# One attention and gated-MLP kernel on one core: the planner that writes out its order gets a model of the DMA link

## The chip, the cores and the metric

The kernel runs on one core of one Trainium2 chip. The metric is the device time of one execution in microseconds (us). Its engines are TensorE (PE, with its weight loads as PEld), VectorE (DVE), ScalarE (ACT), GpSimd (POOL) and SyncE (SP). Each runs its own instructions in the order in which they stand. SP and POOL also issue the transfers (DMA), so a transfer's place in the order of its queue decides when it can start.

## The reference, cut to what matters

```python
# q, k, v: (8, 8, 576, 64); s: (8, 8, 576)
scores = scale * np.matmul(q, k.transpose(0, 1, 3, 2))
cum = np.cumsum(np.maximum(s, 0.0), axis=-1)
bias = -(cum[:, :, :, None] - cum[:, :, None, :])
scores = np.where(causal, -1e9, scores + np.minimum(bias, 0.0))
attn = softmax(scores)                       # with 1e-9 added to the sum
x = heads joined of np.matmul(attn, v)       # (8, 576, 512)
h = np.maximum(x @ w_in, 0.0)                # (8, 576, 1024)
u, v = h[..., :512], h[..., 512:]
v_n = (v - mean(v)) / np.sqrt(var(v) + 1e-6)
v_s = np.einsum('ts,bsd->btd', w_spatial, v_n) + b_spatial
out = (u * v_s) @ w_out
```

## The kernel before, in words

Every matrix product is made of float16 products: an operand is split into a high and a low half, and three products (high-high, high-low, low-high) are added in PSUM. The 64 heads are worked as 32 pairs, four pairs to a batch entry. For each pair `s_pass` makes the scores in seven or eight groups of matmuls, masks them and finds the smallest negated score on VectorE, takes exponentials on ScalarE, and splits the weights into `pb` (two heads of 4 blocks of rows each) and `pbt` (the last 64 rows of both heads). A DMA transpose on SP's queue turns each into `pT` (2 buffers' worth per pair, 4 buffers) and `pTt`. `av_pass` multiplies them with V: 30 + 30 matmuls into the one bank `psV`, 30 into `psT`. The four pairs of a batch entry fill `xt`, on which `mlp` does four stages: `xt` by the second half of `win` with a layer norm over features, the first half of `win`, the spatial product (`vn` by `ws`) and the output product (`g` by `wo`).

Pairs 0 to 2 take q and k as float32 ("native", in the tiles `g` and `xt`). For pairs 3 to 31 `load_raw` fetches `raw` on POOL's queue (576 KB), and `split_raw` makes the halves: ScalarE writes `KA`, GpSimd writes `QB` by subtraction, and SP's queue does five copies. In the order of the program they are `QA <- KA`, `KB <- KA`, `KB <- QB`, `QB <- KA`, and last the prefix sums `KA <- dr_cc`. `QB <- KA` overwrites the half of `QB` that `KB <- QB` reads, and `KA <- dr_cc` overwrites three rows of `KA` that `QB <- KA` reads, so each stands on SP's queue until the one before it has landed, and what is behind it stands too. The weights come in through POOL's queue too (`fetch_win`, 512 KB each) into buffers that later hold other things (`vn`, `g`, `u`, `wst`), and are taken apart on VectorE.

No instruction's place is written by hand. `Recorder.add` records each operation with a cost from `Recorder.cost` (time on its engine, `occ`, and time until its result is there, `lat`) and its predecessors from `Recorder.touch`. `Recorder.schedule` is a list scheduler: it walks a modelled clock, takes on each engine the ready operation of the lowest `prio` (a position that the plan at the end of `attn_gated_mlp` gives: scores of pair p at 2p, its `av_pass` at 2p + 3.7, the MLP of batch b from 8b + 10.3), and the order in which it took them is the order of each engine's instructions. The modelled clock is used for nothing else: on the chip only the order and the semaphores count. Since all instructions are issued by the wrapper, they carry one line number (L247).

Of the kernel before, what the change touches and what calls it, by code (L numbers as in the profile page):

```python
# [24 lines left out]
BYTES = {F32: 4, U32: 4, F16: 2, BF16: 2}  # L25
# [4 lines left out]


class Op:
    __slots__ = ("eng", "calls", "occ", "lat", "port", "preds", "succs", "prio", "n")


class Recorder:
    WAKE = {"vector": 30, "scalar": 30, "tensor": 50, "gpsimd": 85, "sync": 60}

    def __init__(self):
# [38 lines left out]
    def add(self, eng, method, args, kw):  # L78
        merge = isinstance(self.open, Op)
        if merge:  # L80
            op = self.open
            assert op.eng == eng
        else:
            op = Op()
            op.eng, op.calls, op.occ, op.lat, op.port = eng, [], 0.0, 0.0, False
            op.preds, op.succs, op.n = {}, [], len(self.ops)
            op.prio = self.prio
            self.ops.append(op)
            if self.open == "new":
                self.open = op  # L90
        op.calls.append((method, args, kw))
        is_ap = lambda x: hasattr(x, "ap") and hasattr(x, "tensor")
        writes = [x for k, x in kw.items() if k in ("out", "accum_out") and is_ap(x)]
        reads = [x for k, x in kw.items() if k not in ("out", "accum_out") and is_ap(x)]
        if args:
            rest = [x for x in args if is_ap(x)]
            if "out" in kw:
                reads += rest
            else:
                writes.append(rest[0])  # L100
                reads += rest[1:]
        occ, lat, port = self.cost(eng, method, writes, reads, kw, op)
        op.lat = max(op.lat, op.occ + lat)
        op.occ += occ
        op.port = op.port or port
        for w, aps in ((False, reads), (True, writes)):
            for ap in aps:
                r = self.region(ap)
                if r is not None:
                    self.touch(op, r, w)  # L110

    def touch(self, op, r, w):
        name, p0, p1, f0, f1 = r
        log = self.access.setdefault(name, [])
        kept = []
        for e in log:
            q0, q1, g0, g1, other, ow = e
            hit = q0 < p1 and p0 < q1 and g0 < f1 and f0 < g1
            if hit and (w or ow) and other is not op:
                data = ow and not w  # L120
                op.preds[other] = op.preds.get(other, False) or data or other.eng != op.eng
            if w and p0 <= q0 and q1 <= p1 and f0 <= g0 and g1 <= f1 and other is not op:
                continue
            if not w and not ow and other is op and e[:4] == (p0, p1, f0, f1):
                continue
            kept.append(e)
        kept.append((p0, p1, f0, f1, op, w))
        self.access[name] = kept

    def cost(self, eng, method, writes, reads, kw, op):  # L130
        size = lambda ap: ap.size() // ap.shape[0]
        n = max([size(a) for a in writes + reads] or [1])
        ps = any(a.tensor.name in self.psum for a in reads)
        point = any(size(a) == 1 for a in reads) and n > 1
        if method == "dma_start_transpose":
            return 1.26 * n + 60, 1.26 * n + 60 + 2500, False
        if method == "dma_start":
            b = max(a.size() * BYTES[a.dtype] for a in writes)
            o = 600
            return o, o + (2300 if eng == "sync" else 2800) + b / 180.0, False  # L140
        if eng == "tensor":
            n = size(writes[0])
            f32 = reads[0].dtype == F32
            t = n * (4 if f32 else 1) / 2.4 + 2.5
            t = max(t, 27.0)
            w = writes[0]
            key = (size(w), self.region(w)[1], w.shape[0])
            last = getattr(op, "calls")[-2:-1]
            if last and w.shape[0] == 64 and key[1] == 64:
                lw = last[0][1][0]  # L150
                if size(lw) == n and lw.shape[0] == 64 and self.region(lw)[1] == 0:
                    t = 3.0
            return t, t + 180, False
        if eng == "vector":
            if method == "tensor_tensor_reduce":
                return n / .96 + 76, n / .96 + 200, False
            if method == "reciprocal":
                return 85, 172, False
            if method == "bn_aggr":
                return 98, 180, False  # L160
            if method == "bn_stats":
                return n / .96 + 72, n / .96 + 152, False
            if n <= 16:
                return 75, 155, False
            big = [a for a in reads if size(a) > 16]
            if method == "memset":
                return n / .96 + 10, n / .96 + 80, False
            if method in ("tensor_copy", "tensor_scalar") and not ps:
                o = n / 1.92 + (195 if point else 75)
                return o, o + 80, True  # L170
            o = n / .96 + (130 if point and not ps else 72)
            return o, o + 80, len(big) > 1 and not ps
        if eng == "scalar":
            o = n / 1.2 + (50 if ps else 98) + (90 if point else 0)
            if len(writes) > 1:
                return o + 93, o + 200, False
            return o, o + 95, False
        if eng == "gpsimd":
            if method == "tensor_tensor":
                o = 560 if n < 16 else n * 1.9 + 150  # L180
            elif method == "memset":
                o = n * .86 + 80
            else:
                o = 260 if n < 16 else n * .9 + 150
            return o, o + 90, True
        raise ValueError((eng, method))

    def schedule(self):


        left = {}
        for op in self.ops:
            left[op] = len(op.preds)
            for p in op.preds:
                p.succs.append(op)
        free = dict.fromkeys(self.WAKE, 0.0)
        soon = {e: [] for e in free}
        ready = {e: [] for e in free}
        start = {}
        at = dict.fromkeys(self.ops, 0.0)  # L200
        port = 0.0
        for op in self.ops:
            if not left[op]:
                heapq.heappush(soon[op.eng], (0.0, op.n, op))
        order = []
        while len(order) < len(self.ops):
            best = None
            for e in free:
                t = free[e]
                while soon[e] and soon[e][0][0] <= t:  # L210
                    _, _, op = heapq.heappop(soon[e])
                    heapq.heappush(ready[e], (op.prio, op.n, op))
                if not ready[e]:
                    if not soon[e]:
                        continue
                    t = soon[e][0][0]
                    if best is not None and t >= best[0]:
                        continue
                if best is None or t < best[0]:
                    best = (t, e)  # L220
            t, e = best
            while soon[e] and soon[e][0][0] <= t:
                _, _, op = heapq.heappop(soon[e])
                heapq.heappush(ready[e], (op.prio, op.n, op))
            _, _, op = heapq.heappop(ready[e])
            s = t
            if op.port:
                s = max(s, port)
                port = s + op.occ
            start[op] = s  # L230
            free[e] = s + op.occ
            order.append(op)
            for o in op.succs:
                data = o.preds[op]
                when = s + op.lat + self.WAKE[o.eng] if data else s + 1
                at[o] = max(at[o], when)
                left[o] -= 1
                if not left[o]:
                    heapq.heappush(soon[o.eng], (at[o], o.n, o))
        self.start = start  # L240
        return order
# [612 lines left out]
```

## Time and profile before

| | |
|---|---|
| median of 3 runs | 744.07 us (741.94 to 750.85) |
| the profiled execution: time, span | 744.18 us, 742.5 us |
| granted TensorE clock, mean | 0.915 |
| PE busy | 619.3 us (83%) |
| DVE busy | 555.7 us (75%) |
| ACT busy | 516.0 us (69%) |
| POOL busy | 189.6 us (26%) |
| DMA moved | 119.30 MB, mean 161 GB/s |
| SP's queue, share of 16 DMA engines | 58.6% |
| POOL's queue, share of 16 DMA engines | 17.2% |

A busy share is an average over a start of about 240 us, in which weights and the first pairs come in, and a long middle in which TensorE is nearly full. So the table is read by stretches. "Issue to landing" of a transfer runs from its issue on the queue to the semaphore that says it is there.

### The profile page before, as it was taken

How to read it: one execution, taken by the hardware profiler on the slowest of the kernel's cores; microseconds unless marked ns; L12 is line 12 of the kernel's file. 1: busy time of each engine (PE TensorE's matmuls, PEld its weight loads, DVE VectorE, ACT ScalarE, POOL GpSimd, SP SyncE). 2: the span in 40 equal slices, each digit the busy share in tenths (PEclk: the TensorE clock that was granted, in tenths of full speed). 3: DMA queues.
4: the chain of work that ended last, by engine and by line, in shares of the span. 5: the costliest groups of instructions: out<-in, count | busy, mean ns of one | idle time of the engine just before them, and what ended most of it. 6: DMA issues, size and time to landing. Idle time of an engine off the chain costs nothing.

```text
span 742.5 us, 15798 instructions
## 1 busy us (share of the span) xinstructions
PE 619.3 (83%) x5696; PEld 427.1 (58%) x5696; DVE 555.7 (75%) x1602; ACT 516.0 (69%) x1328; POOL 189.6 (26%) x303
## 2 busy tenths in 40 slices
PE   4605445898559898998997999989999989999997
PEld 2202223466336476756775667657765777677676
DVE  7818697868966697978994988788877988984331
ACT  4626667566868496977895888778886978783322
POOL 7404223311422321233121331232233212100100
PEclk9857555989759999999998999999999999999999
DMA  8897677738679898898889687968897779564101
GB/s 227 244 164 172 145 154 163 174 63 180 174 142 213 185 163 183 173 226 159 193 171 190 137 197 160 255 141 184 153 241 170 180 144 196 100 115 87 43 2 64
DMA packets 237413, 119.30 MB, mean 161 GB/s; under 512 B 213864, under 2 KB 217110, under 8 KB 237335
## 3 DMA queue, kind: packets, MB, share of 16 engines
q1 hardware_dynamic: 228039, 83.23, 58.6%
q0 software_dynamic: 9296, 35.07, 17.2%
q8 instruction: 44, 0.72, 0.4%
q14 instruction: 34, 0.28, 0.1%
HBM read 37.48 MB, written 9.66 MB: 63 GB/s over the span
## 4 chain that ended last, share of the span: by engine, by line
PE 46%; DMA 16%; DVE 12%; ACT 8%; issue 2%; SPq 0%; POOL 0%; ACTq 0%; DVEq 0%; POOLq 0%
PE psM L247 33%; DMA pT<-pb 11%; PE psV L247 6%; PE psS L247 5%; DMA pTt<-pbt 3%; DVE psS L247 3%; ACT pb L247 2%; DVE pb L247 2%; PE psT L247 2%; DVE g L247 2%; ACT p L247 2%; DMA st<-st 1%; DVE pbt L247 1%; ACT q L247 1%; DVE st L247 1%
## 5 line engine op out<-in xcount | busy, mean ns | idle before, releaser
L247 DVE SCALAR_TENSOR_TENSOR pb<-p,sm,pb 128x384 f16<-128x384 f32 (+3 forms) x256 | 139.6, 582 | 36.5 <-ACT pb L247 35.9
L247 DVE CUSTOM_DVE_ANT_0 psS<-psS,mb 128x128 f32<-128x128 f32 (+2 forms) x295 | 142.6, 495 | 17.8 <-PE psS L247 14.0
L247 ACT ACTIVATE pb<-p,sm 128x384 f16<-128x384 f32 (+3 forms) x256 | 127.3, 553 | 30.5 <-DMA pT<-pb 17.8
L247 POOL TENSOR_TENSOR QB<-raw,KA 128x288 f16<-128x288 f32 x116 | 90.6, 807 | 207.5 <-ACT KA L247 207.2
L247 ACT ACTIVATE p<-psS,mx 128x128 f32<-128x128 f32 (+1 forms) x236 | 123.0, 527 | 29.4 <-DVE sm L247 17.6
L247 PEld LDWEIGHTS <-V 128*64 128x64 f16 x1920 | 82.6, 123 | 83.5 <-issue 73.8
L247 PE MATMUL psV<-pT,V 128*64 128x128 f16 (+2 forms) x960 | 78.7, 313 | 52.5 <-DMA pT<-pb 52.5
L247 PE MATMUL psM<-ws,vn 128*128 128x288 f16 x768 | 107.0, 287 | 0.0
L247 PE MATMUL psS<-KA,QA 128*128 128x512 f16 (+1 forms) x336 | 80.1, 315 | 29.4 <-ACT q L247 14.9
L247 PE MATMUL psM<-xt,win 128*128 128x288 f16 x768 | 101.1, 288 | 3.9 <-ACT u L247 3.6
L247 PE MATMUL psM<-g,wo 128*128 128x288 f16 x768 | 103.0, 288 | 1.6 <-DVE g L247 1.6
L247 PE MATMUL psM<-win,xt 128*128 128x512 f16 (+1 forms) x576 | 102.4, 354 | 0.8 <-ACT hv L247 0.5
L247 PEld LDWEIGHTS <-win 128*128 128x128 f16 x768 | 74.6, 98 | 27.0 <-issue 5.6
L247 PEld LDWEIGHTS <-wo 128*128 128x128 f16 x768 | 74.8, 98 | 25.1 <-issue 2.4
L247 PEld LDWEIGHTS <-vn 128*128 128x128 f16 x768 | 74.0, 98 | 24.3 <-issue 2.1
L247 PE MATMUL psS<-KB,QB 128*128 128x512 f16 (+1 forms) x336 | 87.1, 312 | 0.0
L247 PEld LDWEIGHTS <-xt 128*128 128x128 f16 (+1 forms) x576 | 48.0, 105 | 48.3 <-issue 6.5
L247 ACT ACTIVATE xt<-psV 128x512 f16<-128x512 f32 x32 | 19.1, 596 | 54.2 <-PE psV L247 54.2
L247 POOL TENSOR_SCALAR rs<-mv 128x1 f32<-128x1 f32 x40 | 8.8, 221 | 182.4 <-DVE mv L247 118.4
L247 PEld LDWEIGHTS <-QB 128*128 128x128 f16 x348 | 30.1, 105 | 41.1 <-issue 30.7
L247 DVE SCALAR_TENSOR_TENSOR xt<-psV,xt 128x512 f16<-128x512 f32 x32 | 21.9, 685 | 39.9 <-ACT xt L247 39.7
L247 ACT ACTIVATION_READ_ACCUMULATOR p<-psS,mx 128x1 f32 x236 | 47.8, 203 | 0.0
(112 smaller groups left out, 894.6 us busy)
## 6 DMA issues: line engine op xcount, KB each, us to landing
raw<-in_qkT_dram POOLq DMA_DIRECT2D x29, 576.0 KB, 5.8
out_dram<-ob SPq DMA_DIRECT2D x32, 288.0 KB, 4.7
vraw<-in_v_dram POOLq DMA_DIRECT2D x16, 512.0 KB, 6.8
QA<-KA SPq DMA_DIRECT2D x29, 144.0 KB, 3.1
KB<-KA SPq DMA_DIRECT2D x29, 144.0 KB, 4.0
KB<-QB SPq DMA_DIRECT2D x29, 144.0 KB, 6.4
QB<-KA SPq DMA_DIRECT2D x29, 144.0 KB, 2.8
vraw<-in_v_dram POOLq DMA_DIRECT2D x16, 128.0 KB, 6.4
```

The costliest lines, as they stand in the source:

```text
L247: getattr(eng, method)(*args, **kw)
```

## The change

The scheduler gets a model of one link that all transfers share. A transfer has a size in time, `op.dma`: its bytes over a rate of 0.22, 0.26 or 0.3 bytes per ns, for a transpose, a load of an input, or any other copy. When the scheduler takes a transfer, the link's end moves on by that time; the queue that issues is held when the link is more than 4 us behind; and the result counts as there only at the link's end plus a fixed reserve (`SLACK`: 8, 6 or 4.5 us). Before, a transpose was there 2.5 us after its own cost, a copy about 2.3 or 2.8 us plus bytes over 180 per ns, and transfers did not know of each other. Last, when an operation overwrites what an earlier transfer of the same queue reads or writes, the model now lets it wait until that transfer is done; before, only the start counted.

Nothing else differs: the same operations on the same engines, with the same buffers, semaphore rules and priorities.

```diff
+    SLACK = dict(turn=8000, load=6000, copy=4500)
+    RATE = dict(turn=0.22, load=0.26, copy=0.3)
...
+        if method.startswith("dma"):
+            kind = "turn" if "transpose" in method else "load" if any(
+                a.tensor.name.startswith("in_") for a in reads) else "copy"
+            op.dma = max(a.size() * BYTES[a.dtype] for a in writes) / 1e0 / self.RATE[kind] / 1e3
...
-                op.preds[other] = op.preds.get(other, False) or data or other.eng != op.eng
+                op.preds[other] = op.preds.get(other, False) or data or other.eng != op.eng or other.dma > 0
...
-            return 1.26 * n + 60, 1.26 * n + 60 + 2500, False
+            return 1.26 * n + 60, self.SLACK["turn"], False
...
-            b = max(a.size() * BYTES[a.dtype] for a in writes)
-            o = 600
-            return o, o + (2300 if eng == "sync" else 2800) + b / 180.0, False
+            load = any(a.tensor.name.startswith("in_") for a in reads)
+            return 600, self.SLACK["load" if load else "copy"], False
...
+            done = s + op.lat
+            if op.dma:
+                link = max(link, s + min(op.occ, 600)) + op.dma
+                if link > s + op.occ + 4000:
+                    free[e] = link - 4000
+                done = max(done, link + op.lat)
...
-                when = s + op.lat + self.WAKE[o.eng] if data else s + 1
+                when = done + self.WAKE[o.eng] if data else s + 1
```

How it moves instructions is shown at three places (all lines are the recorder's one issuing line, L247 before and L260 now).

**POOL's queue at the start.** `vn`, `g`, `wst` and `u` are the buffers into which the weights of `w_in` are loaded; `QB_75` and `QB_76` belong to the first two pairs that are split. Before:

```order
L247 DMA vn_89<-in_w_in_dram 128x1024
L247 TENSOR_TENSOR QB_75<-raw_98,KA_72 128x288
L247 DMA vraw_100<-in_v_dram 128x4x256
L247 DMA vraw_100<-in_v_dram 128x256
L247 TENSOR_TENSOR QB_75<-raw_98,KA_72 128x288 x3
L247 DMA raw_99<-in_qkT_dram 128x1152
L247 DMA g_94<-in_w_in_dram 128x1024
L247 DMA g_95<-in_w_in_dram 128x1024
L247 DMA wst_97<-in_w_in_dram 128x1024
L247 DMA u_96<-in_w_in_dram 128x1024
L247 DMA raw_98<-in_qkT_dram 128x1152
L247 DMA u_96<-in_w_in_dram 128x1024
```

and now:

```order
L260 DMA vn_89<-in_w_in_dram 128x1024
L260 DMA raw_99<-in_qkT_dram 128x1152
L260 DMA g_94<-in_w_in_dram 128x1024
L260 DMA vraw_100<-in_v_dram 128x4x256
L260 DMA vraw_100<-in_v_dram 128x256
L260 TENSOR_TENSOR QB_75<-raw_98,KA_72 128x288 x4
L260 DMA g_95<-in_w_in_dram 128x1024
L260 DMA wst_97<-in_w_in_dram 128x1024
L260 DMA u_96<-in_w_in_dram 128x1024
L260 TENSOR_TENSOR QB_76<-raw_99,KA_73 128x288 x4
L260 DMA raw_98<-in_qkT_dram 128x1152
L260 DMA u_96<-in_w_in_dram 128x1024
```

Of seven loads that stood behind each other, two (`raw_99`, `g_94`) now stand ahead of the subtractions of `QB_75`, and two (`raw_98` and the second `u_96`) behind those of `QB_76`.

**TensorE at the first `av_pass`.** `psV` is its result; the matmuls of `xt1_0` and `xt1_1` are scores of pair 2. Before:

```order
L247 MATMUL psM2_66<-xt1_0_92,xt1_1_93 128x384
L247 MATMUL psS1_62<-xt1_0_92,xt1_1_93 128x128
L247 MATMUL psS1_62<-xt1_0_92,xt1_1_93 128x384
L247 LDWEIGHTS V1_0_81
L247 MATMUL psV0_67<-pT0_105,V1_0_81 64x384
```

and now:

```order
L260 MATMUL psM2_66<-xt1_0_92,xt1_1_93 128x384
L260 MATMUL psS1_62<-xt1_0_92,xt1_1_93 128x128
L260 MATMUL psS1_62<-xt1_0_92,xt1_1_93 128x384
L260 MATMUL psM0_64<-xt1_0_92,xt1_1_93 128x256
L260 MATMUL psS2_63<-xt1_0_92,xt1_1_93 128x256
L260 MATMUL psS2_63<-xt1_0_92,xt1_1_93 64x128 x2
L260 MATMUL psM1_65<-xt1_0_92,xt1_1_93 128x512
L260 LDWEIGHTS V1_0_81
L260 MATMUL psV0_67<-pT0_105,V1_0_81 64x384
```

The first `av_pass` has moved behind three more groups of scores. The same holds later: each `av_pass` stands one or two score groups and some MLP chunks further back, and the `psT` part no longer follows the `psV` part at once.

**SP's queue in the middle.** Buffers 1 of `KA`, `KB` and `QB` belong to one pair's copies; `pT3` and `pTt1` are another pair's transposes. Before:

```order
L247 DMA KB1_79<-KA1_73 64x1152
L247 DMA KB1_79<-QB1_76 64x1152
L247 DMA QB1_76<-KA1_73 64x1152
L247 DMA KA1_73<-dr_cc_146 3x2x576
L247 DMA_TRANSPOSE pT3_108<-pb1_104 128x20x128
L247 DMA_TRANSPOSE pTt1_111<-pbt0_112 128x10x128
L247 DMA_TRANSPOSE pT0_105<-pb0_103 128x20x128
```

and now:

```order
L260 DMA KB1_79<-KA1_73 64x1152
L260 DMA KA0_72<-dr_cc_146 3x2x576
L260 DMA KB1_79<-QB1_76 64x1152
L260 DMA_TRANSPOSE pT3_108<-pb1_104 128x20x128
L260 DMA_TRANSPOSE pTt1_111<-pbt0_112 128x10x128
L260 DMA QB1_76<-KA1_73 64x1152
L260 DMA out_0_dram<-ob0_121 128x576
L260 DMA_TRANSPOSE pT0_105<-pb0_103 128x20x128
L260 DMA out_0_dram<-ob1_122 128x576
L260 DMA KA1_73<-dr_cc_146 3x2x576
```

The transposes have moved ahead of the two copies that wait for a copy before them, and the last of these, `KA1 <- dr_cc`, now stands behind three transposes instead of ahead of them.

## Rows read from the trace of the kernel before

**Rows 1.** Windows, four stages: length, busy us per engine, TensorE's granted clock, DMA.

```profile
0.00:120.00 120.00, 54.51 (x332) 28.26 (x332) 86.81 (x215) 68.33 (x160) 46.41 (x68) 0.70 0.84 184
120.00:240.00 120.00, 92.05 (x788) 60.51 (x785) 92.55 (x260) 85.16 (x217) 32.87 (x49) 0.83 0.73 156
240.00:640.00 400.00, 374.60 (x3684) 264.79 (x3683) 328.22 (x995) 316.72 (x836) 105.04 (x172) 0.98 0.87 179
640.00:742.50 102.50, 98.19 (x902) 73.55 (x900) 48.12 (x133) 45.76 (x119) 5.32 (x14) 1.00 0.31 66
```

**Rows 2.** Waits of TensorE, 0 to 240 us: total, times, longest.

```profile
PE psV L247 <- DMA pT<-pb: 32.2, 7, 16.1
PE psS L247 <- ACT q L247: 20.6, 6, 6.1
...
PE psT L247 <- DMA pTt<-pbt: 6.6, 3, 3.0
```

**Rows 3.** Waits of TensorE, 240 to 640 us.

```profile
PE psV L247 <- DMA pT<-pb: 20.3, 13, 4.2
PE psM L247 <- ACT u L247: 3.6, 4, 1.5
```

**Rows 4.** Timeline, 20 to 52.5 us: start, length, idle before in brackets.

```profile
25.22 0.55 POOL L247 DMA_DIRECT2D raw<-in_qkT_dram  x1
...
25.59 14.30 SPq L247 DMA_TRANSPOSE pT<-pb  x1
...
25.77 1.06 POOL L247 DMA_DIRECT2D g<-in_w_in_dram  x2
...
26.81 0.54 POOL L247 DMA_DIRECT2D wst<-in_w_in_dram  x1
...
27.34 0.54 POOL L247 DMA_DIRECT2D u<-in_w_in_dram  x1
27.85 0.54 POOL L247 DMA_DIRECT2D raw<-in_qkT_dram  x1
28.38 0.54 POOL L247 DMA_DIRECT2D u<-in_w_in_dram  x1
...
51.28 0.48 PE L247 MATMUL psV<-pT,V 128*64 128x384 f16 x1 [16.10 <-DMA pT<-pb]
```

**Rows 5.** DMA issues: KB each, median us from issue to landing.

```profile
raw<-in_qkT_dram POOLq DMA_DIRECT2D x29, 576.0 KB, 5.8
...
KB<-QB SPq DMA_DIRECT2D x29, 144.0 KB, 6.4
QB<-KA SPq DMA_DIRECT2D x29, 144.0 KB, 2.8
...
g<-in_w_in_dram POOLq DMA_DIRECT2D x3, 512.0 KB, 6.6
```

**Rows 6.** The tile pT: its 64 transposes, issue to landing.

```profile
DMA to landing us min/median/max: 4.8/5.2/25.7
```

**Rows 7.** Timeline of SP's queue, 438 to 500 us.

```profile
447.38 0.59 SPq L247 DMA_DIRECT2D KB<-QB  x1
453.30 0.46 SPq L247 DMA_DIRECT2D QB<-KA  x1
455.59 0.24 SPq L247 DMA_DIRECT2D KA<-dr_cc  x1
455.93 3.34 SPq L247 DMA_TRANSPOSE pT<-pb  x1
```

**Rows 8.** Waits of SP's queue, 240 to 640 us.

```profile
SPq L247 <- DMA KB<-QB: 57.3, 14, 5.6
...
SPq L247 <- DMA QB<-KA: 31.9, 16, 4.1
```

**Rows 9.** Windows of 10 us at the start; columns as in the first group.

```profile
30.00:40.00 10.00, 5.18 (x16) 1.91 (x15) 5.21 (x14) 3.55 (x10) 1.29 (x2) 0.84 1.08 308
40.00:50.00 10.00, 0.00 (x0) 0.00 (x0) 0.00 (x0) 0.00 (x0) 0.00 (x0) 0.50 1.21 102
```

More of the change, by code (lines that the diff above doesn't have):

```diff
@@ L32 @@
 class Op:
-    __slots__ = ("eng", "calls", "occ", "lat", "port", "preds", "succs", "prio", "n")
+    __slots__ = ("eng", "calls", "occ", "lat", "port", "preds", "succs", "prio", "n", "dma")
 class Recorder:
+    SLACK = dict(turn=8000, load=6000, copy=4500)
+    RATE = dict(turn=0.22, load=0.26, copy=0.3)
     WAKE = {"vector": 30, "scalar": 30, "tensor": 50, "gpsimd": 85, "sync": 60}
@@ L87, in add @@
             op.prio = self.prio
+            op.dma = 0.0
             self.ops.append(op)
@@ L200, in schedule @@
         at = dict.fromkeys(self.ops, 0.0)
-        port = 0.0
+        port = link = 0.0
         for op in self.ops:
```

## The prediction, made before the changed kernel ran

> **What bounds the kernel now.** I read the windows by stage first, then the waits of TensorE in each stage, then the timeline around its longest wait, and last what SP's queue does ahead of the transposes. The windows [rows 1] show three stages of different kind. Up to 240 us TensorE works 54.5 + 92.1 of 240 us, at a granted clock of 0.70 and 0.83 of full speed: it is starved, while VectorE is busy 86.8 of the first 120 us. From 240 to 640 us TensorE is busy 374.6 of 400 at 0.98, and VectorE 328, ScalarE 317. There TensorE is the bound, and its 25.4 us of idle time are what an order can give back. After 640 us it is busy 98.2 of 102.5, so nothing is left.
>
> The waits say what the idle time is. Before 240 us the `av_pass` waits 32.2 us for `pT` in 7 waits and 6.6 us for `pTt`, beside 20.6 us in which scores wait for ScalarE's exponentials [rows 2]. From 240 to 640 us 20.3 of the 25.4 us are 13 waits for `pT` [rows 3]; the next is ScalarE's `u` with 3.6. So in all 52.5 us of TensorE's idle time are one thing: a matmul placed before its transposed weights have landed. That is what a planner's model of landings acts on.
>
> Two mechanisms make the transposes late. At the start seven loads were issued on POOL's queue between 25.22 and 28.38 us: two of `raw`, five of weights [rows 4]. The transpose issued at 25.59 held SP's queue for 14.3 us, and the `av_pass` got its weights at 51.28, after 16.10 us of idleness. In that hole every engine stands: the window 40 to 50 us has no busy time at all, the DMA share is over 1 and the granted clock 0.50, which is the lower of the two levels [rows 9]. In the middle SP's queue blocks itself. `KB <- QB` was issued at 447.38, `QB <- KA`, which overwrites its source, only at 453.30, `KA <- dr_cc` at 455.59, and the transpose behind them at 455.93 [rows 7]: 8.5 us after the first of the chain. Such waits sum to 57.3 and 31.9 us of SP's time from 240 to 640 us [rows 8].
>
> **The change part by part.** No instruction is added or removed; busy time is the same, and only places move. The sum is made against the profiled execution, 744.2 us (span 742.5 and 1.7 around it), which stands 0.1 us above the median of 744.07.
>
> Term 1, POOL's loads at the start. The seven loads are 2 x 576 + 5 x 512 = 3712 KB [rows 4, 5]. Now two (1088 KB) stand ahead of the four subtractions of `QB_75` and two (1088 KB) behind those of `QB_76`; three are left in one run. The two behind leave 1.11 MB less on the link ahead of the first transposes. From 30 to 50 us the link moved 308 and 102 GB/s, a mean of 205 [rows 9], so that is 5.4 us; the two ahead would give as much again if they got away the 5.8 to 6.6 us earlier that such a load takes to land [rows 5]. That is 10.8 us at best from both, but what is moved behind still has to pass before pair 1's transposes. I take -8 us; ends 0 (the link is only rearranged) and -16.1 (the whole wait).
>
> Term 2, the other waits for `pT` and `pTt` before 240 us: 32.2 - 16.1 + 6.6 = 22.7 us [rows 2]. Each `av_pass` now has more score groups and MLP chunks ahead of it as cover. But here TensorE is not the bound: VectorE's 86.8 of 120 us and the scores' waits for ScalarE are next in line, so most of what is freed is waited for elsewhere. I take a quarter, -5 us; ends 0 and -22.7.
>
> Term 3, the 20.3 us from 240 to 640 us [rows 3]. Two moves act on them together: the transposes stand ahead of `QB <- KA`, so the 8.5 us chain is no longer in front of them, and each `av_pass` stands one or two score groups later. The longest of the 13 waits is 4.2 us, less than that chain. TensorE is nearly full there, so a wait that goes comes off the end. I take two thirds, -13.5 us; ends 0 and -20.3.
>
> Term 4, new waits. `KA <- dr_cc`, the last copy before a pair's scores can start, now stands behind three transposes. A large one occupies the queue 3.34 us [rows 7], so this copy leaves some 7 to 10 us later than in its old place. TensorE shows no wait for it now, so there is slack of unknown size. Also `out_dram <- ob` and the layer norm's small exchange change places with transposes on the same queue. What is queued behind `KA <- dr_cc` on TensorE is everything, as its order is strict. I take +3 us; ends 0 and 1.5 us for each of 29 pairs, +43.5. I take a value near the lower end, because no wait of that kind is among the rows now.
>
> A clock above 0.98 and 0.83 would come on top where the holes close; the cost of that is inside the ranges and not in the sum.
>
> Sum: 744.2 - 8 - 5 - 13.5 + 3 = 720.7 us, so about **721 us**.
>
> **A rule against it.** The planner now counts a load as there after its bytes over 0.26 per ns and 6 us more, which for 576 KB is 8.3 us; the trace has 5.8 [rows 5]. A large transpose is counted at 8 us and 3; the trace has a median of 5.2, a minimum of 4.8 and a maximum of 25.7 [rows 6]. So the reserve is for the tail of the landings, not for the usual one. The Trainium skill, DMA: Bandwidth & Descriptors, section Anatomy of one DMA, goes further: about 2.0 us fixed and the bytes over 436 GB/s, an estimate of 3.4 us for such a load; the trace does not agree, with 5.8. By that rule the reserve would be mostly empty, and the sum would be 744.2 with nothing off.
>
> **The rivals.**
> - *The transposes land as late as before, in other company* (same, 737 us). A copy of 144 KB takes 2.8 us to land as `QB <- KA`, but 6.4 us as `KB <- QB` [rows 5], the one that is issued about when GpSimd has finished with a `raw` buffer and the next 576 KB load starts. The transposes now take the place behind it. If they pay the same 3.6 us, they land after 8.8 instead of 5.2 us and eat most of the later place of the `av_pass`. Term 3 shrinks to a third of its value, term 1 to half, term 2 to nothing: 744.2 - 4 - 4.5 + 1 = 737. For it: a DMA share of 0.87 [rows 1]. Against it: the chain's 8.5 us is larger than 3.6.
> - *Reserves without use* (same, 744 us). Where landings stay near their minimum, a matmul that the plan puts 11 us (8 + 3) behind its transpose gains nothing over one put about 6 us behind it (its old cost and 2.5 us), and the waits that remain are the odd late ones, which no fixed reserve catches. Against it: 13 waits in 400 us are not odd ones.
> - *The hold exists in the plan alone* (729 us). On the chip nothing stops POOL's queue when the link is behind; it issues as soon as the order allows. If the three loads left in a row, with `vraw` ahead and `raw_98` and `u` soon behind, are burst enough, term 1 is nothing: 744.2 - 5 - 13.5 + 3 = 728.7.
> - *The prefix-sum copy becomes the bound* (slower, 761 us). This is the far end of term 4: if `KA <- dr_cc` lands after TensorE has come to the pair's first score group, the whole engine stands for the difference. It decides from the point at which the 7 to 10 us by which it is later exceed its slack. At 1.5 us for 29 pairs: 744.2 - 26.5 + 43.5 = 761. For it: it is the last of five copies on a queue that already waits a great deal. Against it: no wait of TensorE for it in any stage now.
>
> **How the numbers follow.** Chances: the forecast 0.50; landing in other company 0.24; reserves without use 0.07; hold in the plan alone 0.08; the prefix-sum copy 0.11. A measurement of this kernel tells about 2% from no change, that is 14.9 us: below 729.2 is faster, above 759.0 slower. Faster: the forecast with nearly its whole chance and half of the third rival, 0.53. Slower: 0.11. Within 2%: the rest, 0.36. The range begins at 704: the forecast with all of term 3 (7 us more) and all of term 1 (8 us more) is 705.7, and 2 us for the clock. It ends at 748, over the two rivals of no change with some loss; left out are the last rival and the far ends of terms 1 to 3 together, some 2 in 10.
>
> **What would show it.** Right: TensorE's wait for `pT` from 240 to 640 us falls below 8 us; the first `av_pass` starts 5 us or more before 51.28; SP's waits for `KB <- QB` no longer have a transpose right behind them; windows from 240 to 640 us have TensorE busy over 97% of the time. Wrong: a new row in which scores (`psS <- KA,QA`) wait for DMA into `KA`; a median landing of `pT` near 8.8 us with the same waits; the hole between 35 and 51 us of the same length; or the waits gone and TensorE idle as long behind ScalarE or VectorE, which would mean that the middle is less TensorE's than its 374.6 of 400 us says.

## The result, and the profile after

The changed kernel takes 685.06 us, median of 4 runs (681.38 to 686.81), against 744.85 us before (4 runs, 741.94 to 750.85). The ratio is 0.918, 95% interval 0.911 to 0.925: 8.2% faster, where 3.1% was forecast, and below the range of 704 to 748. Some executions take some per cent longer at a lower granted clock; the ratios leave them out, the medians do not.

| profiled execution | before | after |
|---|---|---|
| time, span (us) | 744.18, 742.5 | 686.81, 685.1 |
| PE busy (us) | 619.3 | 609.9 |
| DVE busy (us) | 555.7 | 562.3 |
| granted TensorE clock, mean | 0.915 | 0.943 |

The four stages of the kernel after, which answer to [rows 1]:

```profile
0.00:120.00 120.00, 62.22 (x409) 32.55 (x410) 100.19 (x256) 81.95 (x197) 51.19 (x72) 0.74 0.94 205
120.00:240.00 120.00, 106.15 (x958) 67.82 (x957) 107.49 (x298) 94.97 (x239) 42.35 (x64) 0.93 0.84 184
240.00:640.00 400.00, 400.00 (x4010) 275.61 (x4009) 339.59 (x1019) 324.68 (x862) 99.36 (x161) 1.00 0.86 178
640.00:685.00 45.00, 41.52 (x324) 31.45 (x322) 15.03 (x32) 13.91 (x32) 3.30 (x8) 1.00 0.09 32
```

From 240 to 640 us TensorE is busy all 400 us at the full clock, and the list of its waits there has no row at all, where [rows 3] had 20.3 us for `pT`. (A matmul's end in the profile is modelled, so "busy" says that no gap is seen.) That stage can't be compared by its times, since the kernel after reaches 240 us further on in its work. So both executions are cut at the same work: the start ends where a fifth of TensorE's columns are done, with 1066 matmuls behind it and 4631 or 4632 ahead. Windows of the kernel before, cut there:

```profile
0.00:235.20 235.20, 141.76 (x1066) 85.44 (x1067) 175.34 (x464) 148.95 (x363) 77.99 (x115) 0.76 0.77 169
235.20:738.30 503.10, 477.33 (x4632) 341.66 (x4630) 380.36 (x1139) 366.60 (x966) 111.65 (x188) 0.99 0.76 157
```

and of the kernel after:

```profile
0.00:206.70 206.70, 135.07 (x1066) 79.59 (x1067) 177.71 (x464) 149.40 (x365) 81.96 (x115) 0.81 0.88 193
206.70:681.20 474.50, 474.50 (x4631) 327.83 (x4629) 384.59 (x1139) 365.70 (x964) 114.24 (x188) 1.00 0.79 166
```

The start is 28.5 us shorter and the rest 28.6. In the rest TensorE's idle time went from 25.8 us (503.1 - 477.33) to none, and the same matmuls take 2.8 us less, at a granted clock of 1.00 instead of 0.99.

In the start TensorE's idle time went from 93.4 us (235.2 - 141.76) to 71.6 (206.7 - 135.07), which is 21.8 less, and the same 1066 matmuls take 6.7 us less, at a granted clock of 0.81 instead of 0.76. What TensorE waited for there, before, beside [rows 2] (total, times, longest):

```profile
PE psS L247 <- ACT p L247: 14.7, 10, 3.8
PE psM L247 <- ACT p L247: 8.4, 6, 2.6
```

and after:

```profile
PE psS L260 <- ACT p L260: 20.3, 11, 3.2
PE psV L260 <- DMA pT<-pb: 16.2, 2, 12.3
PE psM L260 <- ACT p L260: 13.2, 6, 6.9
PE psS L260 <- ACT q L260: 8.8, 5, 3.2
```

The waits for `pT` and `pTt` fell from 38.8 us (32.2 + 6.6) to 16.2. All other idle time stayed: 54.6 us before (93.4 - 38.8), 55.4 after (71.6 - 16.2). So what was freed was not waited for elsewhere.

VectorE tells the same from its side. It does the same 464 instructions in 175.3 and 177.7 us; what went is its idle time, 59.9 us before (235.2 - 175.34) and 29.0 after (206.7 - 177.71).

What VectorE waited for in the start, before (0 to 235 us: total, times, longest):

```profile
DVE xt L247 <- ACT xt L247: 24.4, 8, 6.6
DVE pb L247 <- ACT pb L247: 18.6, 3, 16.8
```

and after (0 to 207 us):

```profile
DVE pb L260 <- ACT pb L260: 11.6, 4, 10.3
DVE sm L260 <- ACT p L260: 4.8, 3, 2.6
DVE xt L260 <- ACT xt L260: 2.8, 3, 2.0
```

`pb` and `xt` reach VectorE through ScalarE, and ScalarE's own waits before, in the same stretch, say for what:

```profile
ACT xt L247 <- PE psV L247: 28.4, 8, 7.1
ACT pb L247 <- DMA pT<-pb: 17.8, 1, 17.8
```

`xt` is drained from `psV`, so its wait is the wait for an `av_pass`: for the transposes, and for the `av_pass`'s own matmuls. Behind the first hole TensorE waited 16.1 us for `pT` (32.2 - 16.1), so at most that much of the 24.4 us is the transposes' lateness. Nearly all of the 24.4 us went.

On SP's queue the chain of copies stands in the new order. The kernel after, 400 to 432 us:

```profile
402.69 0.47 SPq L260 DMA_DIRECT2D KB<-QB  x1
406.09 3.68 SPq L260 DMA_TRANSPOSE pT<-pb  x1
410.08 1.33 SPq L260 DMA_TRANSPOSE pTt<-pbt  x1
411.47 0.69 SPq L260 DMA_DIRECT2D QB<-KA  x1
...
417.73 0.27 SPq L260 DMA_DIRECT2D KA<-dr_cc  x1
```

Where `QB <- KA` used to hold the queue [rows 7], two transposes leave. The waits of [rows 8], 57.3 and 31.9 us, have no row in the list of SP's waits from 240 to 640 us any more; the largest there is now for VectorE's `pb`, 53.8 us in 25 waits.

The first `av_pass` takes its first matmul from one head's transpose and its second from the other's. In the kernel before the first line is the last of [rows 4], and behind it stands

```profile
54.56 3.14 PE L247 MATMUL psV<-pT,V 128*64 128x384 f16 x27 [2.80 <-DMA pT<-pb]
```

In the kernel after:

```profile
40.42 0.53 PE L260 MATMUL psV<-pT,V 128*64 128x384 f16 x1
53.25 3.04 PE L260 MATMUL psV<-pT,V 128*64 128x384 f16 x25 [12.30 <-DMA pT<-pb]
```

Its first matmul starts 10.9 us earlier and no longer waits, but the second has to wait until 53.25, only 1.3 us earlier than before. Its transpose takes as long from issue to landing as the first one did before: after, SP's queue holds the two transposes for 24.86 us, and the chain of waits has the second of them with 25.25 us, where [rows 6] has a longest landing of 25.7.

```profile
23.91 24.86 SPq L260 DMA_TRANSPOSE pT<-pb  x2
```

```profile
27.96 25.25 DMA pT<-pb
```

So the hole is still there. It is now shorter on VectorE (10.3 instead of 16.8 us in the rows above), because more of its work stands in front: it is busy 9.96 us from 30 to 40 us, where [rows 9] has 5.21.

### The profile page after: what moved, and what is told of

Its sections match the earlier page's. It is cut to its first block, busy times and chain, and to the rows that moved or that the text cites. A ratio compares the mean times of both kernels' runs of the same rounds, so it can differ in the third digit from the quotient of the medians.

```text
span 685.1 us, 15839 instructions
## 1 busy us (share of the span) xinstructions
PE 609.9 (89%) x5696; PEld 407.4 (59%) x5696; DVE 562.3 (82%) x1602; ACT 515.5 (75%) x1328; POOL 196.2 (29%) x303
## 4 chain that ended last, share of the span: by engine, by line
PE 78%; DVE 9%; DMA 5%; ACT 5%; issue 2%; POOL 1%; ACTq 0%; DVEq 0%; POOLq 0%
PE psM L260 57%; PE psS L260 11%; PE psV L260 8%; DMA pT<-pb 4%; DVE pb L260 2%; PE psT L260 2%; DMA vraw<-in_v_dram 1%; ACT p L260 1%; DVE psS L260 1%; DVE ob L260 1%; ACT pb L260 1%; DVE psM L260 1%; POOL QB L260 1%; DVE V L260 1%; DVE hv L260 1%
## 5 line engine op out<-in xcount | busy, mean ns | idle before, releaser
L260 DVE CUSTOM_DVE_ANT_0 psS<-psS,mb 128x128 f32<-128x128 f32 (+2 forms) x295 | 143.5, 495 | 20.6 <-PE psS L260 16.0
L260 DVE SCALAR_TENSOR_TENSOR pb<-p,sm,pb 128x384 f16<-128x384 f32 (+3 forms) x256 | 141.7, 588 | 20.5 <-ACT pb L260 20.3
L260 ACT ACTIVATE p<-psS,mx 128x128 f32<-128x128 f32 (+2 forms) x236 | 123.0, 526 | 25.7 <-DVE mx L260 18.0
L260 ACT ACTIVATE pb<-p,sm 128x384 f16<-128x384 f32 (+3 forms) x256 | 126.4, 555 | 12.1 <-DMA pT<-pb 11.8
L260 POOL TENSOR_TENSOR QB<-raw,KA 128x288 f16<-128x288 f32 x116 | 94.2, 837 | 125.8 <-ACT KA L260 125.3
L260 PE MATMUL psM<-ws,vn 128*128 128x288 f16 x768 | 107.7, 286 | 0.0
L260 PE MATMUL psM<-g,wo 128*128 128x288 f16 x768 | 105.2, 290 | 0.5 <-POOL wo L260 0.5
L260 PE MATMUL psM<-win,xt 128*128 128x512 f16 (+1 forms) x576 | 103.7, 354 | 0.9 <-ACT p L260 0.9
L260 PE MATMUL psM<-xt,win 128*128 128x288 f16 x768 | 100.3, 286 | 0.9 <-ACT u L260 0.9
L260 PE MATMUL psS<-KA,QA 128*128 128x512 f16 (+1 forms) x336 | 80.1, 314 | 21.2 <-ACT p L260 17.7
L260 PEld LDWEIGHTS <-V 128*64 128x64 f16 x1920 | 67.0, 116 | 46.7 <-issue 36.1
L260 PEld LDWEIGHTS <-wo 128*128 128x128 f16 x768 | 74.9, 99 | 27.0 <-issue 2.9
L260 PEld LDWEIGHTS <-win 128*128 128x128 f16 x768 | 73.7, 98 | 23.8 <-issue 3.2
L260 PEld LDWEIGHTS <-vn 128*128 128x128 f16 x768 | 73.3, 98 | 24.6 <-issue 2.9
L260 PE MATMUL psS<-KB,QB 128*128 128x512 f16 (+1 forms) x336 | 86.1, 308 | 0.0
L260 PE MATMUL psV<-pT,V 128*64 128x384 f16 (+2 forms) x960 | 65.6, 292 | 16.2 <-DMA pT<-pb 16.2
L260 PEld LDWEIGHTS <-xt 128*128 128x128 f16 (+1 forms) x576 | 46.8, 105 | 49.6 <-issue 9.2
L260 POOL TENSOR_SCALAR rs<-mv 128x1 f32<-128x1 f32 x40 | 11.4, 285 | 173.0 <-DVE mv L260 139.8
L260 PEld LDWEIGHTS <-QA 128*128 128x128 f16 x348 | 29.8, 103 | 38.6 <-issue 30.4
L260 ACT CAST g<-g 128x288 f16<-128x288 f32 x64 | 27.2, 428 | 32.0 <-DVE g L260 31.8
L260 PEld LDWEIGHTS <-QB 128*128 128x128 f16 x348 | 30.1, 104 | 30.9 <-issue 24.3
L260 ACT ACTIVATION_READ_ACCUMULATOR p<-psS,mx 128x1 f32 x236 | 47.8, 202 | 0.0
```

The costliest lines, as they stand in the source:

```text
L260: getattr(eng, method)(*args, **kw)
```

## The experiments

All edits are to the plan alone, but for the fifth. In the table "start" is the time at which a fifth of TensorE's columns are done, "idle" VectorE's idle time in it, and "rest" what follows up to about TensorE's last matmul; these three are of one profiled execution each. Ratios are to the kernel before, measured beside each. The runs were not all on one chip, and the median of the kernel before beside them was 738.5 to 744.9 us, so runs of different groups are compared by their ratios.

| run | plan | median us | ratio (95%) | start | idle | rest |
|---|---|---|---|---|---|---|
| before | | 744.85 | 1 | 235.2 | 59.9 | 503.1 |
| changed | | 685.06 | 0.918 (0.911-0.925) | 206.7 | 29.0 | 474.5 |
| 1 | transposes' reserve alone | 751.08 | 1.012 (1.005-1.020) | 223.2 | 51.1 | 519.1 |
| 2 | overwriting wait alone | 716.39 | 0.966 (0.960-0.972) | 227.5 | 53.4 | 484.8 |
| 3 | changed, no overwriting wait | 735.95 | 0.996 (0.991-1.001) | 213.1 | 37.4 | 514.2 |
| 4 | changed, no hold | 691.74 | none given | 192.3 | 15.2 | 477.2 |
| 5 | before, chain on POOL's queue | 724.78 | 0.977 (0.970-0.984) | 222.8 | 45.7 | 496.2 |
| 6 | changed, small reserves | 684.99 | 0.922 (0.914-0.930) | 204.0 | 28.8 | 478.9 |
| 7 | changed, no link | 705.30 | 0.951 (0.945-0.958) | 213.8 | 36.3 | 480.6 |
| 8 | overwriting wait, transposes' reserve | 712.71 | 0.961 (0.954-0.969) | 223.2 | 45.9 | 483.2 |
| 9 | overwriting wait, three late landings | 734.65 | 0.994 (0.988-0.999) | 225.0 | 48.1 | 499.6 |
| 10 | changed, middle reserves | 683.74 | 0.925 (0.914-0.936) | 211.8 | 33.8 | 473.9 |
| 11 | changed, small reserves, no hold | 694.69 | 0.935 (0.922-0.949) | 213.5 | 37.2 | 489.9 |
| 12 | changed, middle reserves, no hold | 672.67 | 0.913 (0.906-0.920) | 190.7 | 13.6 | 474.7 |
| 13 | overwriting wait, link at the start | 692.32 | 0.936 (0.929-0.944) | 195.4 | 22.9 | 487.2 |
| 14 | overwriting wait, link later | 718.49 | 0.961 (0.951-0.971) | 226.5 | 51.7 | 477.6 |

The profiled executions of runs 10 and 11 were the longest of their four (691.33 and 708.98), and those of 4 and 14 the shortest (675.21 and 709.72); their last three columns are read with that in mind.

**Cover or queue (runs 1 to 3).** The theories: the gain of the middle comes from the `av_pass` standing later on TensorE, or from the transposes standing ahead of the copies that wait on SP's queue.

Run 1:

```diff
-            return 1.26 * n + 60, 1.26 * n + 60 + 2500, False
+            return 1.26 * n + 60, 1.26 * n + 60 + 7700, False
```

> The kernel before, with one number of the plan changed: a large transpose counts as there 5.2 us later (7.7 us after its own cost, 2.5 before). SP's queue keeps its order of copies (21 of 29 chains with the two waiting copies back to back before, 24 here), POOL's queue keeps its run of nine transfers at the start. Theory cover (the gain of the middle comes from av_pass standing later, behind more matmuls): 744 less about 28, the gain after a fifth of TensorE's work, is 716, or 706 with some of the start. Theory queue (it comes from the transposes standing ahead of the copies that wait): 738 to 745, with waits for pT left from 240 us on.

Run 2:

```diff
-                op.preds[other] = op.preds.get(other, False) or data or other.eng != op.eng
+                op.preds[other] = op.preds.get(other, False) or data or other.eng != op.eng or any(
+                    c[0].startswith("dma") for c in other.calls)
```

> The kernel before, with only the wait of an overwriting transfer put into the plan. SP's queue is reordered (the two waiting copies stand back to back in 5 of 29 chains instead of 21); av_pass stands where it stood on TensorE. Theory cover: 738 to 745, waits for pT as before. Theory queue: 706 to 716, and most of the 20.3 us of waits for pT from 240 to 640 us gone. If both matter, about 730.

Run 3, from the changed kernel:

```diff
-                op.preds[other] = op.preds.get(other, False) or data or other.eng != op.eng or other.dma > 0
+                op.preds[other] = op.preds.get(other, False) or data or other.eng != op.eng
```

> The changed kernel, with only the wait of an overwriting transfer taken out of the plan: 27 of 29 chains have the two waiting copies back to back again; av_pass stands as late as in the changed kernel, POOL's loads as spread. Theory cover: 685 to 690, TensorE still without a wait for pT from 240 us on. Theory queue: 705 to 714, the middle's 28 us lost again.

The cover theory falls in all three: cover alone is slower (751), the wait alone gives 0.966, and the change without it gives nothing (0.996). In run 3's profile the start is 22.1 us shorter than before all the same and the rest 11.1 us longer: most of what the change does in the start needs no overwriting wait, what it does in the rest does. Run 1 shows why cover doesn't pay. TensorE's waits from 240 to 640 us in run 1:

```profile
PE psM L247 <- ACT ob L247: 11.6, 3, 6.6
PE psM L247 <- ACT hv L247: 9.7, 5, 4.3
PE psV L247 <- DMA pT<-pb: 4.7, 4, 2.4
```

The wait for `pT` did fall, from 20.3 to 4.7 us, and 21.3 us of waits for ScalarE took its place. One of them in run 1's chain of waits:

```profile
539.10 9.35 DMA out_dram<-ob
...
548.47 0.42 ACT ob L247
548.89 0.04 issue
548.93 2.77 PE psM L247 x24
```

ScalarE stands until an output store lets go of its buffer; behind it on ScalarE stand the evacuations that free TensorE's banks. That SP's queue made this store late is not shown. It left right behind a transpose and took 9.35 us from issue to landing, where the median of these stores is 4.7 in the kernel before. The queue does stand a great deal in run 1 (64.4 us of waits for `KB <- QB` from 240 to 640 us), and in run 8, which is run 1 with the overwriting wait, TensorE has no wait for `ob` in that stretch. In run 2 the two largest waits of TensorE in that stretch are

```profile
PE psV L248 <- DMA pT<-pb: 7.9, 6, 2.5
PE psM L248 <- ACT u L248: 3.3, 4, 1.5
```

20.3 us became 7.9, and this run changes next to nothing but the order of SP's queue. By operation and tile, 127 of SP's 351 instructions in the trace stand at another place; ScalarE's and GpSimd's all stand where they stood, VectorE's but for 6 of 1602 and TensorE's matmuls but for 12 of 5696.

**The chain off SP's queue (run 5).** The wait itself stays; another queue stands for it.

```diff
-        Y.dma_start(out=QB[i][hi], in_=KA[i][lo])
-        Y.dma_start(out=KA[i][61:64], in_=ccd[2 * p:2 * p + 2].rearrange("h r s -> r h s"))
+        G.dma_start(out=QB[i][hi], in_=KA[i][lo])
+        G.dma_start(out=KA[i][61:64], in_=ccd[2 * p:2 * p + 2].rearrange("h r s -> r h s"))
```

> The kernel before, old plan and all, but the copies QB <- KA and KA <- dr_cc are issued from POOL's queue instead of SP's. TensorE's order is the one of before, so av_pass has no more cover. Theory queue (SP's queue standing behind KB <- QB makes transposes and stores late): as much as the overwriting wait in the plan gave or more, 705 to 722, and the waits for pT from 240 us on down from 20 to below 10. Rival (the stall only moves: POOL stands 8 us per chain instead, its layer-norm scalars and loads come late): 735 to 755.

724.78 us lies between the two, with the sign of the queue theory: TensorE's waits for `pT` from 240 to 640 us fell from 20.3 to 5.6 us, by a move of two copies, with all but 22 of TensorE's matmuls at the same place. Whether it gives less than run 2 is barely shown (the intervals, 0.970 to 0.984 and 0.960 to 0.972, overlap a little), and why is open; TensorE has 20.5 us of idle time in the rest here, 13.9 in run 2.

**What gives the other 31 us (runs 4, 6, 7, 8).** From 716 to 685 us (by ratio 0.966 to 0.918) it is the hold, the reserves, the link, or cover once the queue no longer stands.

Run 4 takes out of the changed plan

```diff
-                if link > s + op.occ + 4000:
-                    free[e] = link - 4000
```

> The changed kernel, with only the hold of the issuing queue taken out of the plan (the link is still modelled): POOL's longest run of transfers is nine again instead of five. Theory burst (the 11 us by which the first av_pass came earlier are from the spread loads): the first av_pass near 51 us again, and 692 to 700 in all. If the burst is covered by other work now, or the start is given back later: 683 to 689.

Run 6 changes one line of it:

```diff
-    SLACK = dict(turn=8000, load=6000, copy=4500)
+    SLACK = dict(turn=2500, load=2200, copy=1700)
```

> The changed kernel with the reserves cut to 2.5, 2.2 and 1.7 us; link, hold and overwriting wait stay, av_pass stands about where it stood before (18.8 us of matmul cost behind its last scores, 17.9 before, 24.2 changed). If the reserve is what the link and the overwriting wait lack for the last 31 us: 712 to 720, as with the overwriting wait alone. If the link is: 685 to 695.

Run 7 takes each transfer by itself, and the hold goes with the link:

```diff
-                link = max(link, s + min(op.occ, 600)) + op.dma
-                if link > s + op.occ + 4000:
-                    free[e] = link - 4000
-                done = max(done, link + op.lat)
+                done = max(done, s + min(op.occ, 600) + op.dma + op.lat)
```

> The changed kernel with each transfer still at its own rate, but none behind another: reserves and overwriting wait stay, the hold is gone. If the reserves do the rest of the work: 683 to 695. If the shared link does: 712 to 720.

Run 8 has the edits of runs 1 and 2 together.

> The kernel before with two things only: the overwriting wait and the large transpose's reserve (7.7 us). Alone the first gave 24 us and the second cost 9. If the reserve pays once SP's queue no longer stands (cover works when the transposes leave in time): 690 to 705, no wait for pT from 240 us on. If the two are independent: about 725.

The large reserves are not needed: with small ones the ratio is 0.922, with the change's 0.918, and the intervals overlap widely. The link is: without it and the hold the ratio is 0.951. Run 7's start is still 13.7 us shorter than run 2's, so each transfer's own rate and large reserves do a part of the same work where no link does it. Run 8 can't be told from run 2 (0.961 and 0.966), so cover does little even with a free queue.

In run 4 the first `av_pass` came at 50.3 us, which is the burst theory's number, but not for its reason: TensorE has no wait for `pT` up to 240 us there, the `av_pass` only stands further back. Three of its four executions took 690.68 to 694.12 us and the profiled one 675.21, too far apart for a ratio, so that the hold is worth nothing is not shown either. Its nine transfers do leave in one run again, but from 13.22 us on, where seven of those of before left between 25.22 and 28.38, and its first two transposes hold SP's queue for 8.48 and 7.80 us, not for 14.30 and 11.33 as before. So a gain in the start needs no spreading of POOL's loads by the hold. Whether loads that leave earlier give some of it was not tried by itself.

**Where the link earns it (runs 9, 13, 14).** Run 9 told the plan of run 2 by hand what the trace of before had measured for the first transposes:

```diff
-            return 1.26 * n + 60, 1.26 * n + 60 + 2500, False
+            late = 22500 if len(self.ops) < 110 else 2500
+            return 1.26 * n + 60, 1.26 * n + 60 + late, False
```

> The kernel before with the overwriting wait, and one thing more: the plan counts the first two large transposes and the first small one as there 20 us later than it did, which is what the trace of before measured (25.7 us from issue to landing). Nothing models a link; POOL's run of nine transfers stays. Theory filled hole (the start gains because the plan puts VectorE's and ScalarE's other work into the hole before the first av_pass, which needs no spread of the loads): VectorE's hole of 17.6 us shrinks below 8, a fifth of TensorE's work is done by about 212 instead of 227.5, and 696 to 705. Theory spread loads: 712 to 720, as with the overwriting wait alone.

That prediction fell: 734.65. The hole at 35 to 52 us closed, and one of 19 us opened at 57.7. TensorE's longest wait of the start in run 9:

```profile
PE psS L249 <- DMA KA<-dr_cc: 28.9, 1, 28.9
```

With three landings late and the rest on time, the plan put the copies of the next pair behind them, and scores that need `KA <- dr_cc` ahead. It closes one hole and opens another, so it doesn't decide the matter. Runs 13 and 14 switch the whole link on for a part (the edit of run 2, and link, hold and small reserves for some transfers; `op.res` is the small reserve):

```diff
...
+            done = s + op.lat
+            if op.dma and op.prio < 18:      # run 14: op.prio >= 18
+                link = max(link, s + min(op.occ, 600)) + op.dma
+                if link > s + op.occ + 4000:
+                    free[e] = link - 4000
+                done = max(s + op.res, link + op.res)
```

> The kernel before with the overwriting wait, and the link with small reserves and hold for the transfers of plan positions below 18 alone (about the first fifth of TensorE's work); later transfers as before. If the link earns its time in the start by closing VectorE's holes: start about 204 to 212 us instead of 227.5, VectorE idle there 29 to 37 us instead of 53, the rest 480 to 486 as with the overwriting wait alone, 690 to 700 in all. If it earns it in the middle: 712 to 720.

> The counterpart: overwriting wait everywhere, link with small reserves and hold only from plan position 18 on. If the link earns its time in the start: start 225 to 230 us, the rest 478 to 486, 706 to 717 in all. If in the middle: 690 to 700.

The gain lies at the start. Windows of run 13, start and rest:

```profile
0.00:195.40 195.40, 126.05 (x1066) 77.31 (x1067) 172.46 (x464) 148.13 (x365) 82.34 (x115) 0.83 0.93 203
195.40:682.60 487.20, 472.22 (x4631) 336.39 (x4630) 380.92 (x1139) 364.71 (x965) 114.12 (x188) 1.00 0.77 162
```

and of run 14:

```profile
0.00:226.50 226.50, 140.29 (x1066) 81.68 (x1067) 174.84 (x464) 149.13 (x363) 79.56 (x115) 0.76 0.80 174
226.50:704.10 477.60, 470.43 (x4631) 332.64 (x4630) 380.82 (x1139) 367.23 (x966) 117.22 (x188) 1.00 0.78 166
```

With the link at the start alone the start is 32 us shorter than in run 2 (195.4 for 227.5) and the rest 2 us longer; with the link later the start stays (226.5) and the rest is 7 us shorter. By ratio run 13 (0.936) is clear of run 2 (0.966); run 14 (0.961) is not. Together the two differences would make 673 us of start and rest, where run 6, with the link everywhere, has 682.9, so the halves add up only roughly.

In run 13 five loads in a row leave POOL's queue at 24.97 to 27.08 us, much as before, so it shows better than run 4 that the start's gain does not need them spread. Its first transposes are issued earlier, at 21.50 us instead of run 2's 26.39, and its first `av_pass` starts at 44.9 instead of 52.9.

Start less idle is 172 to 178 us in every row of the table, VectorE's own work. That is an account and no proof that VectorE sets the time: on TensorE the same start of run 13 is 69.4 us idle and 126.1 busy, at a granted clock of 0.83, where run 2 has 87.4 idle and 140.1 busy at 0.76.

**In search of a better version (runs 10 to 12).** Reserves between those of the change and the small ones,

```diff
-    SLACK = dict(turn=8000, load=6000, copy=4500)
+    SLACK = dict(turn=5000, load=4000, copy=3000)
```

with the hold (run 10) and without it (run 12), and the small ones without it (run 11).

> The changed kernel with reserves of 5, 4 and 3 us, between those of the change and those of the run with small ones, which came out alike (685). If the size of the reserve doesn't matter once link and overwriting wait are there: 680 to 690. If there is an optimum between (TensorE waits 13.4 us for KA <- dr_cc at the start with small reserves, 3.1 with large ones): 670 to 679.

> The changed kernel with the small reserves and without the hold of the issuing queue: the link and the overwriting wait alone. If the hold does nothing: 681 to 690. If it is the spread of POOL's loads that needs no reserve: 695 to 710.

> The changed kernel with reserves of 5, 4 and 3 us and without the hold. The profiled run without the hold (large reserves) was the fastest of all, 675, with the other three at 691 to 694. If the hold costs the start VectorE's time: 672 to 682; if that one run was chance: 684 to 694.

Run 12 has the lowest time of all: 672.67 us, four runs from 671.07 to 672.97. But the kernel before took 738.51 us beside it, not 744.85, and by ratio it is 0.913 against the change's 0.918, with intervals that overlap widely (0.906 to 0.920, 0.911 to 0.925). So that it is better than the change is not shown. Its windows, start and rest:

```profile
0.00:190.70 190.70, 127.12 (x1066) 76.22 (x1067) 177.12 (x464) 149.66 (x367) 78.36 (x115) 0.84 0.92 211
190.70:665.40 474.70, 474.28 (x4631) 328.50 (x4630) 380.63 (x1139) 363.68 (x961) 120.96 (x188) 1.00 0.79 165
```

VectorE idles 13.6 us in its start. What the hold does has no rule here: taken away, the ratio goes from 0.922 to 0.935 with small reserves and from 0.925 to 0.913 with middle ones, both with overlapping intervals, and with large ones the runs scatter over both sides. Neither sign is shown.

## Why the prediction was wrong, point by point

The direction was right and so were the two places: SP's queue blocking itself, and the first transposes. Two steps failed. In the start it was the **discount in term 2**, "most of what is freed is waited for elsewhere". In the rest it was the **two thirds of term 3**, a size. Beside them stands a term put at nothing, "busy time is the same".

The parts of the miss can be added up. For the start 13 us were forecast (terms 1 and 2) and 28.5 measured: 9.6 more of the waits for `pT` and `pTt`, 6.7 of shorter busy time, less 0.8 of other idle time. For the rest 10.5 were forecast (terms 3 and 4) and 28.6 measured: 6.8 more of the waits for `pT`, 5.5 of other idle time, 2.8 of shorter busy time, and the 3 of term 4.

- *Term 1* (-8 us, fewer loads ahead of the first transposes): the mechanism was half right at most. The first transpose of the pair is there in time for 40.42 instead of 51.28, but the second one lands at 53.25, against 54.56 before, after 25.25 us. What got shorter is the wait in front of it, since more scores stand there.
- *Term 2* (-5 us): "most of what is freed is waited for elsewhere", since VectorE and ScalarE were next in line. VectorE's 86.8 of 120 us [rows 1] were read as a near bound. But it was idle 59.9 of the 235.2 us of the start, and 43.0 of these were `xt` and `pb`, which hang on the same transposes and `av_pass`. So the holes of TensorE and VectorE were in large part one hole. Of the 38.8 us of waits for `pT` and `pTt` 22.6 went, and TensorE's other idle time stayed (54.6 and 55.4 us). Runs 2 and 13 show that the link in the plan does most of this, with small reserves; how much of it is earlier landing and how much other work put into the hole is not told apart.
- *The clock*: "the cost of that is inside the ranges and not in the sum". The same matmuls took 9.5 us less in all (619.35 and 609.88), 6.7 of them in the start at a granted clock of 0.81 for 0.76.
- *Term 3* (-13.5 us): the mechanism held, the size did not. It measured 28.6. All of TensorE's idle time went, not two thirds, and the 5.5 us that were not put down to `pT` went too, with the 2.8 us of faster matmuls. The prediction let both moves act together; the runs give the larger part to the queue's order (run 2, 18.3 us of the rest) and show that cover without it makes the rest 16 us longer (run 1).
- *Term 4* (+3 us): nothing in the rest. But the price exists: the kernel after has one wait of 3.1 us for `KA <- dr_cc` at the start, run 6 two of 13.4 together, run 9 one of 28.9. The slower rival was a real mechanism, of which this order has little.
- *The rule against it*: the reserves are indeed not needed (run 6), as the trace's median landings of 5.2 and 5.8 us suggested. After, a `raw` load lands in a median of 5.4 us. The Trainium skill, DMA: Bandwidth & Descriptors, section Anatomy of one DMA, would have it more strongly, with about 2.0 us and the bytes over 436 GB/s, an estimate of 3.4 us for such a load; the trace after does not agree either, with 5.4. The rates of 0.22 to 0.3 bytes per ns ahead of the prediction are a slip of the unit: the code divides by 1000 once more, so that they are 220 to 300 bytes per ns, and the 8.3 and 3 us are worked out with these. What was wrong was to take the reserve for the change: a result with nothing off was inferred from the one part of three that does little.
- *The rivals*: transposes that land later in other company would have shown a median near 8.8 us; it is 5.7, so that cost is 0.5 us and not 3.6 as far as the trace tells. It has the landing of 26 of the 64 transposes before and of 10 after, and the one of 25.25 us is not among them; the 6.4 us from which this rival was priced is the landing of one `KB <- QB` of 29. The hold in the plan alone was close for the place it spoke of: three weight loads left in a row at 24.42 to 25.49 us, and the transposes held the queue for 24.86 us.
- *The signs*: all four signs of being right came out, with a time that was far off. The start of the first `av_pass` said little, since one matmul of it could start without the other head's transpose.
- *The range*: it left out the far ends of terms 1 to 3 as a rare coincidence. They sum to 744.2 - 16.1 - 22.7 - 20.3 = 685.1. That the time came out there is luck: the first two ends, 38.8 us, measured 28.5, and the third, 20.3, measured 28.6. What is not luck is that they went together. The prediction itself put nearly all the waits behind terms 1 to 3 down to one thing, a matmul placed before its transposed weights have landed, and yet discounted and added them as if they were independent.

## What to carry to other kernels

Before a wait is discounted because another engine is "next in line", ask what that engine waits for in the same stretch: compare the stretch's length with its busy time, and if its holes are the same holes, the whole wait is to be had. In a planner, the order of a queue that stands at its first waiting transfer was worth more here than the place of the consumer: a transfer that waits for another should not stand ahead of ones that are ready, and a plan that knows this in part (late landings without the queue's waits, or three late landings without the rest) can be worse than one that knows less. Terms of a sum with one cause are not added as independent ones, and the range has to reach to all of them at once.

## What the runs showed that was not expected

One late transfer is seen far away: in run 1 an output store issued at 539.10 us was waited for by ScalarE until 548.45 and cost TensorE 6.6 us in one wait. And plans that differ only in the reserves or the hold differ in their start without a rule (190.7 to 213.5 us among six with link and overwriting wait). Single executions of one such plan scatter by about as much (675.21 to 694.12 us in run 4, 686.23 to 708.98 in run 11), so a difference of that size between two of them says little about the rule that made it.
